# The first w_in part is converted between chunk 0's and chunk 1's steps, and the planner judges orders by five cases and another clock

## The chip, the core and the metric

The kernel runs on one core of one Trainium2 chip. The time is the device time of one execution in microseconds (us); the time of a version is the median of three executions. One further execution was recorded by the hardware profiler, and all views below come from it.

## What is computed

An attention block with a state per head (RWKV-7) feeds a two-layer network:

```python
# batch 4, heads 8, 768 tokens, head size 40; all float32
for t in range(S):
    y[:, :, t] = einsum('bhd,bhde->bhe', r_t, state)
    Sa = einsum('bhde,bhe->bhd', state, a_t)
    state = state * w_t[..., None, :] - outer(Sa, b_t) + outer(v_t, k_t)
x = y laid out as 3072 tokens x 320
h = x @ w_in                 # 320 x 2048, float64
out = (h * sigmoid(h)) @ w_out   # 2048 x 320, float64
```

The two weight matrices arrive as 64-bit floats, so the kernel has to turn them into float32 itself, out of their 32-bit halves.

## The kernel before

**Chunks.** The 768 tokens are cut into 12 chunks of 64. For each chunk `prepare` forms the decays by two scans on VectorE (L627, L645) and scales k, b and a by them (L654, L664); TensorE (PE) then makes two triangular products per head (L682) and turns the keys (L769). A triangular matrix has to be inverted per chunk. For chunks 0 to 2 `special` does that: the product goes to DRAM (`ms`) and back (`xs`), VectorE inverts 16 x 16 blocks with pairs of a multiply (L795) and a reduction (L796), the result goes through DRAM again (`zs`, L881) into the tile `mi` (L887, eight transfers), and PE finishes with L926, L913 and six groups of L958, each of which waits for a VectorE addition (L973). Later chunks are inverted in pairs by `inverse` and `merge` (L1039, L1068). `chain` solves for the chunk's updates (L1135, L1166), carries the state to the next chunk (L1223, L1239, L1111, L1121, L1196), `read` forms the chunk's output (L1269, L1281, L1308, L1323, L1334), and `moe` does the network for its 256 tokens: L1405 and L1418 against w_in, a SiLU on ScalarE (L1428), L1445 against w_out.

**Weights.** `weights(n)` converts one part of a weight matrix; parts 0 to 3 and the side tile `wi3` are w_in, the other five w_out. A part is fetched by GpSimd's queue (L479) into a borrowed buffer (`gts`, `wo`, `raw`, `XI`). VectorE and ScalarE then take the words apart: L484 (VectorE), L485 (ScalarE), L486 and L487 (VectorE), L488 (ScalarE). For the first three parts ScalarE also scales the low words (L502), PE adds the halves by four matmuls against the identity (L508), two trace matmuls for each, and VectorE multiplies the sum in (L520). The rest do the sum on VectorE (L493, L500). GpSimd's fetches are held back by small copies (L853) that wait for a given tile, so that loads come in a chosen order.

**Order.** Every step is added to a `Plan` with an engine, a cost, the tiles that it reads and writes, and a priority `pri` (lower is earlier). `Plan.order` lists the steps: at each point it takes the step that can start first, with `pri` weighed in. `Plan.best` draws ten settings and then tries 400 random shifts of priorities; each listing is judged by `Plan.through`, which walks it once per case of `CASES` and returns the end, and the listing with the smallest sum of ends is issued. Engines execute in that order, with semaphores between them; a step that waits holds everything behind it on its own engine. `through` also holds a model of how PE's instructions are fetched in blocks of 256 and of PE's clock by windows of 3.41 us. So a change to the cases or to one priority can shift any step of the whole program.

The priorities that matter here: chunk 0's inverse has -13 and its chain -12, chunk 1's `prepare` -8, its inverse -7, and weights have 1 and more.

Of the kernel before, what the change touches and what calls it, by code (L numbers as in the profile page):

```python
# [33 lines left out]
class Plan:  # L34
# [32 lines left out]
    RATE, LAND = 300.0, 2.0  # L67
    COLD = 42.0
    URGE = {"SP": 0.0, "ACT": 0.03, "PE": 0.05, "DVE": 0.1, "POOL": 0.02}
    LEAVE = {"F": 0.09, "R": 0.2, "T": 0.13, "Q": 0.13, "H": 0.12, "S": 0.11}  # L70
    ENTER = {"F": 0.08, "R": 0.1, "T": 0.03, "Q": 0.03, "H": 0.03, "S": 0.03}

    def turn(self, op):

        a, b = self.shape, op["shape"]
        if a == b or {a, b} == {"R", "T"}:
            return 0.03 if a != "F" else 0.0
        return self.LEAVE[a] + self.ENTER[b]

# [90 lines left out]
            out.append(op)  # L170
        return out

    SLOW = 2.8, 1.7
    CASES = (1.0, 300.0, 0.15, 1.0), (1.5, 240.0, 0.15, 1.0), (1.5, 240.0, 0.25, 1.04)
    WINDOW, FEW = 3.41, 0.42

    def through(self, out, crowd, rate, hop, slower):

        at = dict.fromkeys(self.HOP, 0.0)
        queue = dict.fromkeys(("SP", "ACT", "POOL"), 0.0)
        end, free = [0.0] * len(out), {}
        fetched, count, shape, work = [0.0, 0.0], 0, "Q", {}
        before, after = self.SLOW
        width, few = self.WINDOW, self.FEW
        for op in out:
            e = op["engine"]
            s = at[e]
            for b in op["before"]:  # L190
                s = max(s, end[b] + (hop if self.ops[b]["engine"] != e else 0.0))
            for place in op["takes"]:
                s = max(s, free.get(place, 0.0))
            if e == "PE":
                self.shape = shape
                t, shape = s + self.turn(op), op["shape"]
                to_ = count + op["k"]
                step = op["cost"] / op["k"]
                while count < to_:
                    block = count // 256  # L200
                    gate = 256 * block + 194
                    if len(fetched) == block + 1:
                        full = crowd if max(queue.values()) > t + 1 else 0.0
                        fetched.append(max(t + 0.4, fetched[-1] + before) + after + full)
                    if count >= gate:
                        t = max(t, fetched[-1] + 0.1)
                    to = min(to_, gate if count < gate else 256 * block + 256)
                    left, count = (to - count) * step, to
                    while left > 1e-9:
                        w = int(t / width)  # L210
                        pace = 0.5 if t > 30 and work.get(w - 1, 0.0) < few * width else 1.0
                        d = min((w + 1) * width - t + 1e-9, left / pace)
                        work[w] = work.get(w, 0.0) + d
                        t += d
                        left -= d * pace
            else:
                t = s + op["cost"] * (slower if e == "DVE" else 1.0)
            at[e] = t
            if op["size"]:
                begin, work_ = max(queue[e], t), op["size"] / rate  # L220
                both = max(0.0, max(queue[o] for o in queue if o != e) - begin)
                queue[e] = begin + (2 * work_ if work_ < both / 2 else work_ + both / 2)
                for o in queue:
                    if o != e and queue[o] > begin:
                        queue[o] += min(work_, both / 2)
                t = queue[e] + self.LAND
            end[op["n"]] = t
            for place in op["gives"]:
                free[place] = max(free.get(place, 0.0), t + 0.1)
        return max(end)  # L230

    def best(self, draws, steps):
# [10 lines left out]
        def value(urge, cold, moved):  # L243
# [12 lines left out]
            for op in out:  # L256
                for room in op["rooms"]:
# [4 lines left out]
                    op["gives"].append(place)  # L262
            spans = [self.through(out, *case) for case in self.CASES]
            return sum(spans), out, {i: room.slot for i, room in rooms.items()}
# [24 lines left out]
def kernel(  # L289
# [17 lines left out]
    B, S = v.shape[0], v.shape[1]  # L307
    D, H, P, Q = 40, 8, 4, 16
    DM, DF = w_in.shape[0], w_in.shape[1] // 2
    NF = DF // 128  # L310
    T = B * C
# [53 lines left out]
    few = ZQ.rearrange("p q t -> p (q t)")  # L365
# [8 lines left out]
    def vec(n):  # L374
        return 0.15 + n * 0.00104

    def act(n):
        return 0.19 + n * 0.00082
# [20 lines left out]
    def dma(do, size, r=(), w=(), pri=0, engine="SP", rooms=()):  # L399
        add(engine, 0.45, do, r, w, pri, rooms, size=size)  # L400
# [60 lines left out]
    def weights(n):  # L461
        dst, srcs, key = units[n]
        room = raw[places[n]].bitcast(I32)
        keys = held[places[n]]
        words = room.rearrange("p (c two) -> p c two", two=2)
        lo, hi = words[:, :, 0], words[:, :, 1]
        if len(dst.shape) == 3:
            lo, hi = (x.rearrange("p (k c) -> p k c", k=2) for x in (lo, hi))
        e = dst.bitcast(I32)
        shr, band, bor = ALU.logical_shift_right, ALU.bitwise_and, ALU.bitwise_or  # L470
        pri = (1 if n < 5 else 3) + 0.2 * n
        gate = gates[max(k for k in gates if k <= n)]
        by_pe = n < NP

        def fetch(rows_, src):
            to = room[rows_]
            if len(src.shape) == 3:
                to = to.rearrange("p (g c) -> p g c", g=src.shape[1])
            nc.gpsimd.dma_start(to, src)  # L479

        for n_, (rows_, src) in enumerate(srcs):
            dma(partial(fetch, rows_, src), 1024 / len(srcs), [("@", gate)], [*keys, ("raw", n, n_)], pri, "POOL")
        me = keys
        add("DVE", vec(512), lambda: nc.vector.tensor_scalar(out=e, in0=hi, scalar1=20, scalar2=0x7FF, op0=shr, op1=band), me, key, pri)  # L484
        add("ACT", act(WS), lambda: nc.scalar.activation(out=e, in_=e, func=AF.Relu, scale=2.0**23, bias=low), [], key, pri)  # L485
        add("DVE", vec(WS), lambda: nc.vector.scalar_tensor_tensor(out=e, in0=hi, scalar=-(1 << 31), in1=e, op0=band, op1=bor), me, key, pri)  # L486
        add("DVE", vec(512), lambda: nc.vector.tensor_scalar(out=hi, in0=hi, scalar1=0xFFFFF, scalar2=None, op0=band), [], me, pri)  # L487
        add("ACT", act(WS), lambda: nc.scalar.activation(out=hi.bitcast(F32), in_=hi, func=AF.Copy, scale=2.0**-20, bias=1.0), [], me, pri)  # L488
        if not by_pe:
            add(  # L490
                "DVE",
                vec(WS),
                lambda: nc.vector.scalar_tensor_tensor(  # L493
                    out=hi.bitcast(F32), in0=lo.bitcast(U32), scalar=2.0**-52, in1=hi.bitcast(F32), op0=ALU.mult, op1=ALU.add
                ),
                [],
                me,
                pri,
            )
            add("DVE", vec(WS), lambda: nc.vector.tensor_tensor(out=dst, in0=dst, in1=hi.bitcast(F32), op=ALU.mult), me, key, pri)  # L500
            return
        add("ACT", act(WS), lambda: nc.scalar.activation(out=lo.bitcast(F32), in_=lo.bitcast(U32), func=AF.Copy, scale=2.0**-52), [], me, pri)  # L502
        pf = Room("pair", 5, 1)
        for h in range(2):
            for i in (1, 0):

                def sum_(h=h, i=i):
                    nc.tensor.matmul(  # L508
                        pf.tile[:, h],
                        lhsT=ident,  # L510
                        rhs=words[:, 512 * h : 512 * h + 512, i].bitcast(F32),
                        start=i == 1,
                        stop=i == 0,
                    )

                add("PE", 0.86, sum_, me, [(pf, h)], pri, [pf], 2, shape="F")

        def product():
            f = pf.tile if len(dst.shape) == 3 else pf.tile.rearrange("p a b -> p (a b)")
            nc.vector.tensor_tensor(out=dst, in0=dst, in1=f, op=ALU.mult)  # L520

        add("DVE", vec(WS), product, [(pf, 0), (pf, 1)], key, pri, [pf])
# [955 lines left out]
    for n in range(5):  # L1478
        weights(n)
# [24 lines left out]
    with tc.manual_schedule():  # L1504
# [5 lines left out]
    count = sb.tile([128, 1], F32, name="count")  # L1510
# [7 lines left out]
        out=bad, in0=pb[0:1, 0:1], scalar1=128.0 * 2 * NN - 0.5, scalar2=None, op0=ALU.is_lt  # L1518
# [9 lines left out]
    with tc.If(flag > 0):  # L1528
# [24 lines left out]
        T = 16  # L1553
        with tc.For_i(0, S, T) as t0:
# [3 lines left out]
            for dg in range(4):  # L1558
                for b in range(B):
                    L = slice(32 * dg + H * b, 32 * dg + H * b + H)  # L1560
# [26 lines left out]
        with tc.For_i(0, B * S, 128) as t0:  # L1587
# [12 lines left out]
            for f in range(NF):  # L1600
                ph = gps.tile([128, 512], F32, name="gph", bufs=2)
                F = slice(f * 128, f * 128 + 128)
# [57 lines left out]
```

## Time and profile before

| | |
|---|---|
| median of 3 executions | 743.88 us (742.13 to 744.6) |
| the profiled execution's own time | 742.53 us |
| its span in the profile | 740.8 us |
| mean granted TensorE clock | 0.976 |
| busy: PE, VectorE (DVE), ScalarE (ACT), GpSimd (POOL) | 674.7, 419.5, 194.6, 14.3 us |
| chain that ended last, share of PE | 80% |

PE is busy for 91% of the span. Its rows are listed as time, duration, line, tile and count; an `issue` behind "idle before" is a wait for nothing that the profile shows. A row of PE's shows two matmuls for one matmul of the program, and one for a transpose (L769, L926, L1196), and as many weight loads (PEld). The row `PEclk` is the clock that was granted, as a share of full speed.

### The profile page before, as it was taken

To read this page: it belongs to the slowest core of one execution; us is meant where nothing else is said; L and a number is where in the kernel's file an instruction comes from. 1 tells how busy PE (TensorE), PEld (TensorE's weight loads), DVE (VectorE), ACT (ScalarE), POOL (GpSimd) and SP (SyncE) were. 2 spreads that over 40 slices of the span, in tenths; PEclk is the share of its full clock that TensorE was granted. 3 is DMA by queue.
4 is the path that set the end of the run, shared out by engine and by line. 5 is a ranking of instruction groups with operands and counts; after the bars stand their busy time and mean duration, and the time that the engine had idled before them with its cause. 6 is when DMAs were issued, how large, how long until landed. Compare 5 with 4: busy or idle time off the path is not lost.

```text
span 740.8 us, 27279 instructions
## 1 busy us (share of the span) xinstructions
PE 674.7 (91%) x12666; PEld 540.5 (73%) x12666; DVE 419.5 (57%) x614; ACT 194.6 (26%) x241; POOL 14.3 (2%) x31
## 2 busy tenths in 40 slices
PE   2179799898899999999999999899999999999995
PEld 2176577678678677878778878778777778788773
DVE  6845799976479256299273397362686449321000
ACT  3251635523212411404304205124114211202020
POOL 2300000000000000000000000000000000000000
PEclk9996999999999999999999999999998999999998
DMA  7770654742632453525353506333233321401000
GB/s 248 160 227 11 195 210 126 222 116 47 161 107 58 96 135 98 139 61 125 112 133 106 161 19 144 95 99 92 73 93 81 97 60 32 126 21 41 18 1 22
DMA packets 117979, 77.15 MB, mean 104 GB/s; under 512 B 65506, under 2 KB 114338, under 8 KB 117218
## 3 DMA queue, kind: packets, MB, share of 16 engines
q1 hardware_dynamic: 113352, 64.54, 32.9%
q0 software_dynamic: 2096, 10.49, 4.3%
q8 instruction: 101, 1.65, 0.9%
q10 hardware_dynamic: 2410, 0.30, 0.3%
q14 instruction: 20, 0.16, 0.1%
HBM read 60.29 MB, written 14.61 MB: 101 GB/s over the span
## 4 chain that ended last, share of the span: by engine, by line
PE 80%; DVE 8%; DMA 3%; ACT 3%; issue 3%; SPq 1%; ACTq 1%; DVEq 0%
PE pair L1445 27%; PE pair L1405 21%; PE pair L1418 5%; PE pair L1269 4%; PE pair L682 3%; PE pair L1323 3%; PE pair L958 2%; PE pair L1135 2%; PE pair L1223 2%; PE pair L1068 1%; PE pair L1166 1%; PE pair L508 1%; PE pair L744 1%; PE pair L1308 1%; PE pair L1111 1%
## 5 line engine op out<-in xcount | busy, mean ns | idle before, releaser
L1445 PE MATMUL pair<-wo,gts 128*128 128x320 f32 x768 | 219.8, 442 | 1.1 <-issue 1.1
L1445 PEld LDWEIGHTS pair<-wo,gts 128*128 128x128 f32 x768 | 144.7, 192 | 60.4 <-issue 4.3
L1405 PE MATMUL pair<-xt,wi 128*128 128x256 f32 x768 | 175.5, 386 | 1.6 <-ACT R L756 1.3
L1405 PEld LDWEIGHTS pair<-xt,wi 128*128 128x128 f32 x768 | 145.7, 192 | 24.5 <-ACT R L756 1.4
L1428 ACT ACTIVATE gts<-pair 128x1024 f32<-128x1024 f32 x48 | 46.5, 1020 | 134.5 <-PE pair L1418 108.3
L682 PE MATMUL pair<-a,kb 40*64 40x64 f32 x1536 | 32.2, 236 | 35.8 <-DVE a L654 28.7
L1457 DVE COPY ot<-pair 128x320 f32<-128x320 f32 x24 | 11.8, 490 | 92.4 <-PE pair L1445 88.9
L796 DVE TENSOR_REDUCE XI<-XI 128x64 f32<-128x512 f32 (+9 forms) x85 | 58.6, 690 | 2.9
L682 PEld LDWEIGHTS pair<-a,kb 40*64 40x64 f32 x1536 | 28.6, 149 | 38.5 <-issue 20.5
L1418 PE MATMUL pair<-xt,wi 64*128 64x256 f32 x384 | 47.9, 389 | 0.0
L1281 DVE TENSOR_TENSOR lam<-pair,ml 128x1024 f32<-128x1024 f32 x22 | 26.4, 1220 | 32.9 <-PE pair L1269 30.4
L1418 PEld LDWEIGHTS pair<-xt,wi 64*128 64x128 f32 x384 | 35.1, 187 | 6.7 <-issue 2.6
L795 DVE TENSOR_TENSOR XI<-XI,mi 128x1024 f32<-128x1024 f32 (+8 forms) x60 | 33.6, 559 | 9.6 <-DMA mi<-md 8.3
L1334 DVE TENSOR_TENSOR lam<-pair,wz 128x1024 f32<-128x1024 f32 x11 | 13.5, 1223 | 38.8 <-PE pair L1323 38.8
L1269 PEld LDWEIGHTS pair<-r,vut 40*64 40x64 f32 x1536 | 25.9, 142 | 6.8 <-issue 5.9
L664 DVE TENSOR_TENSOR kb<-kbv 128x512 f32<-128x512 f32 (+1 forms) x36 | 29.7, 861 | 0.3
L1269 PE MATMUL pair<-r,vut 40*64 40x64 f32 x1536 | 28.5, 228 | 1.2 <-issue 1.2
L627 DVE TENSOR_TENSOR_SCAN kbv<-wz,zt 128x1024 f32<-128x1024 f32 x12 | 27.5, 2291 | 0.5
L645 DVE TENSOR_TENSOR_SCAN wz<-wz,zt 128x1024 f32<-128x1024 f32 x12 | 27.5, 2289 | 0.3
L756 ACT COPY R<-pair 128x640 f32<-128x640 f32 x12 | 8.3, 693 | 67.1 <-PE pair L744 61.5
L795 DVE TENSOR_TENSOR XI<-XI,xs 128x1024 f32<-128x1024 f32 (+1 forms) x25 | 25.3, 1010 | 0.8
L407 ACT ACTIVATE vu<-pair 64x640 f32<-64x640 f32 x13 | 9.1, 698 | 60.3 <-PE pair L1135 59.4
(151 smaller groups left out, 687.7 us busy)
## 6 DMA issues: line engine op xcount, KB each, us to landing
wz<-in_wT SPq DMA_DIRECT2D x12, 512.0 KB
kbv<-in_bT SPq DMA_DIRECT2D x12, 512.0 KB
a<-in_aT SPq DMA_DIRECT2D x12, 512.0 KB
kbv<-in_kT SPq DMA_DIRECT2D x12, 512.0 KB
r<-in_rT SPq DMA_DIRECT2D x48, 96.0 KB
vut<-in_vT SPq DMA_DIRECT2D x48, 96.0 KB
vu<-in_v SPq DMA_DIRECT2D x24, 160.0 KB
out<-ot SPq DMA_DIRECT2D x48, 80.0 KB
```

The costliest lines, as they stand in the source:

```text
L627: nc.vector.tensor_tensor_scan(back(V), back(W[:, 2 : 2 + Q * C]), zt, 1.0, ALU.mult, ALU.add)
L645: nc.vector.tensor_tensor_scan(Z, Z, zt, 0.0, ALU.mult, ALU.add)
L664: TTn[engine].tensor_tensor(out=at_(kb, place(is_b, first), (576 * step, 4 // step), (128, 4), (1, C)), in0=blocks((kf, bf)[is_b]), in1=bl ...
L682: nc.tensor.matmul(room.tile[half(b), j, g * C : g * C + C], lhsT=kb[rows(j), place(is_b, q) : place(is_b, q) + C], rhs=A[rows(j), q * C : ...
L795: nc.vector.tensor_tensor(out=at_(tmp, 0, *dims), in0=x, in1=y, op=ALU.mult)
L796: nc.vector.tensor_reduce(out=out_, in_=at_(tmp, 0, *dims), axis=AX.X, op=ALU.add)
L1269: nc.tensor.matmul(pl.tile[half(1 - b if role else b), b, c * C : c * C + C], lhsT=vut[rows(b), role, hu, :], rhs=rs[rows(b), hh, :], star ...
L1281: lambda pl=pl, la=la: nc.vector.tensor_tensor(out=la.tile.rearrange("p (q t) -> p q t", q=Q), in0=pl.tile.rearrange("p a b -> p (a b)").r ...
L1405: nc.tensor.matmul(rooms[g].tile[:, f // 2, (f % 2) * T : (f % 2) * T + T], lhsT=wi[:, k, (4 * g + f) * 128 : (4 * g + f) * 128 + 128], rh ...
L1418: nc.tensor.matmul(rooms[g].tile[:, h, (f % 2) * T : (f % 2) * T + T], lhsT=wi3[half(h), g * 256 + (f % 2) * 128 : g * 256 + (f % 2) * 128 ...
L1428: nc.scalar.activation(out=gts[:, 4 * g * T : 4 * g * T + 4 * T], in_=rooms[g].tile.rearrange("p a b -> p (a b)"), func=AF.Silu)
L1445: nc.tensor.matmul(po[b].tile[:, 0, 0:DM], lhsT=g4[:, f, 128 * b : 128 * b + 128], rhs=wo[:, f, :], start=f == 0, stop=f == NF - 1,)
```

## The change

`weights(0)` gets the priority -8.5 in place of 1: behind chunk 0's steps (-13 to -12) and ahead of chunk 1's `prepare` (-8). The planner's cases go from three to five; each now carries its own two times for fetching PE's instructions, the crowding, the transfer rate, the hop between engines and VectorE's factor. The clock in `through` changes: it now starts at half speed, a window counts at half for work done at half speed, and the share of a window that must be worked is 0.48 to be raised and 0.38 to be kept up, where it was 0.42 of the window before, whatever the clock. Two shapes get a cost for a change of shape that no step here uses.

The kernel does the same operations on the same data; only the order of the engines' instructions differs, over the whole program. On PE one of the four additions of w_in's first part (L508) now stands ahead of chunk 0's L926; three stand behind the chain's L1166 and L1269. The four of the second part stand together behind L1223.

```diff
-    LEAVE = {"F": 0.09, "R": 0.2, "T": 0.13, "Q": 0.13, "H": 0.12, "S": 0.11}
-    ENTER = {"F": 0.08, "R": 0.1, "T": 0.03, "Q": 0.03, "H": 0.03, "S": 0.03}
+    LEAVE = {"F": 0.09, "R": 0.2, "T": 0.13, "Q": 0.13, "H": 0.12, "S": 0.11, "L": 0.13}
+    ENTER = {"F": 0.08, "R": 0.1, "T": 0.03, "Q": 0.03, "H": 0.03, "S": 0.03, "L": 0.03}
...
-    SLOW = 2.8, 1.7
-    CASES = (1.0, 300.0, 0.15, 1.0), (1.5, 240.0, 0.15, 1.0), (1.5, 240.0, 0.25, 1.04)
-    WINDOW, FEW = 3.41, 0.42
-
-    def through(self, out, crowd, rate, hop, slower):
+    CASES = (
+        (2.8, 1.3, 1.0, 300.0, 0.15, 1.0),
+        (2.8, 1.3, 1.0, 300.0, 0.25, 1.0),
+        (2.0, 1.9, 1.0, 240.0, 0.25, 1.0),
+        (2.0, 1.9, 2.0, 240.0, 0.15, 1.0),
+        (1.4, 1.3, 3.0, 300.0, 0.35, 1.05),
+    )
+    WINDOW, FEW = 3.41, (0.38, 0.48)
+
+    def through(self, out, before, after, crowd, rate, hop, slower):
...
-        fetched, count, shape, work = [0.0, 0.0], 0, "Q", {}
-        before, after = self.SLOW
+        fetched, count, shape = [0.0, 0.0], 0, "Q"
+        window, work, pace = -1, 0.0, 0.5
...
-                        pace = 0.5 if t > 30 and work.get(w - 1, 0.0) < few * width else 1.0
+                        if w > window:
+                            known = w == window + 1 and work >= few[pace < 1.0] * width
+                            window, work, pace = w, 0.0, 1.0 if known else 0.5
                         d = min((w + 1) * width - t + 1e-9, left / pace)
-                        work[w] = work.get(w, 0.0) + d
+                        work += d * pace
...
-        pri = (1 if n < 5 else 3) + 0.2 * n
+        pri = -8.5 if n == 0 else (1 if n < 5 else 3) + 0.2 * n
```

The instructions' order on each engine follows from the two programs as they are built; the prediction speaks of these orders. PE, in the first 80 us of before (counts of the program's matmuls): L682 x32 x2, L769 x16 x2, L744 x32, **L682 x32**, L926, L913, **L769 x16**, L958 x16 six times, L1166 x16, L682 x32, L1166 x16, **L769 x16**, L508, L1269 x32 x2, L508 x2, L1323, L1135, L508, L744, L1223, L1196, L1111, L1405 x8. PE after: L682 x32 x2, L769 x16 x2, L744 x32, **L508**, L926, L913, L958 x16 six times, L1166 x16, L682 x32, **L508**, L1166 x16, L1269, L508 x2, L1269, L1135, **L769 x16 x2**, L1323, L1223, **L508 x4**, L682 x32, L1111, L1196, L744, L1405 x8. (Lines are those of the kernel before.)

On VectorE, w_in part 0's L486 and L487 come right behind the last L796 of chunk 0's inverse and ahead of chunk 1's L633 to L664. On ScalarE, L488 comes ahead of the four transfers L887 that ScalarE issues, and L502 right behind them. VectorE's L795 and L796 of chunk 1's inverse, begun before the chain's products in the kernel before, all come behind L1239. On SP's queue, the transfer `zs` (L881) of chunk 1 comes behind eight loads of r and vut and one of a, where it stood behind four loads of r and vut.

## The prediction

> **What bounds the kernel now.** I read the page first: the slices of PE and of its clock.
>
> ```profile
> PE   2179799898899999999999999899999999999995
> PEclk9996999999999999999999999999998999999998
> ```
>
> A slice is 18.5 us. PE is nearly idle in the first two and full from the fifth on, so the end is set by PE's work plus what PE loses, and most of the loss lies ahead of 90 us. The order listings show the same matmuls in both programs; a gain can only be less idle time or less time at half clock. Next the timeline of PE, from where the long idle time ends:
>
> ```profile
> 36.15 1.99 PE L682 MATMUL pair<-a,kb 40*64 40x64 f32 x64 [14.93 <-DVE a L654]
> 38.06 1.12 PE L926 MATMUL pair<-ident,mi 64*128 64x64 f32 x16
> ...
> 46.48 3.31 PE L958 MATMUL pair<-XI 64*64 64x64 f32 x102 [0.99 <-issue]
> 49.65 0.64 PE L1166 MATMUL pair<-X,R 64*40 64x64 f32 x26
> 53.04 0.26 PE L1166 MATMUL pair<-X,R 64*40 64x64 f32 x3 [2.76 <-issue]
> ...
> 56.88 2.07 PE L508 MATMUL pair<-gts,ident 128*128 128x512 f32 x2
> ...
> 74.24 0.60 PE L1196 MATMUL pair<-ident,G 40*104 40x40 f32 x16 [0.92 <-DVE G L1239]
> 77.24 5.33 PE L1405 MATMUL pair<-xt,wi 128*128 128x256 f32 x16 [1.32 <-ACT R L756]
> ```
>
> Two stops have nothing behind them that the profile shows ("issue"). Ahead of the first PE has run 474 matmuls, ahead of the second 602: 128 apart, 256 instructions with the weight loads. So I read them as the fetch of PE's program in blocks of 256. The windows, with the granted clock in the third number from the end, show what the second stop does:
>
> ```profile
> 50.00:53.00 3.00, 0.28 (x18) 0.13 (x6) 0.52 (x1) 0.00 (x0) 0.00 (x0) 1.00 0.36 48
> 53.00:57.00 4.00, 3.96 (x119) 3.72 (x119) 2.99 (x6) 1.20 (x3) 0.00 (x0) 0.53 0.15 37
> 57.00:62.00 5.00, 5.00 (x118) 3.50 (x122) 1.41 (x4) 0.69 (x1) 0.00 (x0) 0.50 0.01 3
> 62.00:67.00 5.00, 5.00 (x46) 2.33 (x40) 3.35 (x11) 0.00 (x0) 0.00 (x0) 0.51 0.01 3
> 77.00:81.00 4.00, 3.76 (x10) 3.05 (x11) 3.75 (x5) 1.85 (x3) 0.00 (x0) 0.57 0.74 210
> ```
>
> PE is full from 54 to 67 us, but at half clock: 13.7 us (53.2 to 66.9), and 3.4 us more after the waits at 74 and 76 us. The four matmuls L508 at 62.50 (two adds) stand right ahead of the return. Last the timelines of VectorE and ScalarE for the steps that the change moves:
>
> ```profile
> 29.83 0.69 DVE L796 TENSOR_REDUCE ZQ<-XI 128x64 f32<-128x512 f32 x1
> 37.75 1.22 DVE L486 SCALAR_TENSOR_TENSOR wi<-gts,wi 128x1024 int32<-128x1024 int32 x1
> 39.00 0.70 DVE L487 TENSOR_SCALAR gts<-gts 128x1024 int32<-128x1024 int32 x1
> ```
>
> ```profile
> 32.36 1.85 ACTq L887 DMA_DIRECT2D mi<-zs  x4
> 43.27 1.15 ACT L488 ACTIVATE gts<-gts 128x1024 f32<-128x1024 int32 x1
> 44.32 1.14 ACT L502 ACTIVATE gts<-gts 128x1024 f32<-128x1024 uint32 x1
> ```
>
> **Step 1, the head of chunk 0's inverse: +0.3 us.** Out of PE's way go L682 (1.99) and a later L769 (1.08), in comes one L508 (2.07 at this clock). But ScalarE now has L488 ahead of the `mi` transfers. L796 ends at 30.5; L486 and L487 follow (1.22 + 0.70), to 32.4; L488 ends at 33.6 in place of an issue at 32.36. The four issues last 1.85, to 35.5, L502 1.14, to 36.6; L508 waits for it and ends at 38.7. Behind L508 are queued L926 and the whole inverse. `mi` itself lands 1.9 after its last issue (as `ms` did: 18.38 to 20.26), at 37, and is not what ends last. L926 starts at 38.7, not 38.06. The gap that L769 filled shrinks, though ScalarE's L675 (1.06 + 0.18) now stands between the copies of X and XI; L958 starts near 42.3, not 42.03. Bounds: -1 if that L508 runs at full clock, +2 if a transfer is late. VectorE's chunk 1 work moves 1.9 later, into its idle 4.0 us ahead of L973; without that cover it would cost the 1.9.
>
> **Step 2, the stops for instructions: -1.1.** The blocks' borders fall elsewhere: what was matmul 474, a third into the L958s, is now matmul 168 of their 192; 602 is in the second L1166. Before, from the end of one block's use (matmul 346, near 40.4) to the release at 46.48 it took 6.1, and from there to 53.04 6.6, while transfers kept the 16 DMA engines full. Now matmul 346 is the 40th of L958, at 43.7; release 49.8. PE is there near 48.2 (168 matmuls in 5.9, by the old pace without its stop): a stop of 1.6. The next point comes after 0.8 + 0.6 + 1.1 + 1.0 + 0.1 of work, at 53.4; the transfers are done by then (0.44 busy at 50 to 52), so I take 54.4: a stop of 1.0, with 0 and 3.0 (the old 6.6) as bounds. Sum 2.6 against 0.99 + 2.76.
>
> [...]
>
> **Step 3, the half clock behind them: -1.7.** A stop of 1.6 in work of small matmuls will, I think, still bring the clock down. Before, the clock came back when two adds (four L508 matmuls) filled most of 3.4 us. Now a single add and then a pair stand earlier, ahead of the second L1269, and should bring it back one such stretch earlier: half of 3.4. Bounds: -6.8 if it is never lost (half of 13.7), +3.1 if it only comes back with the four adds behind L1223 near 73 us (half of 6.1).
>
> [...]
>
> **Step 4, 72 to 82 us: -3.8.** Behind L1223 PE waits 0.92 for G and 1.32 for R, and the following L1405 runs at half clock for 3.4 us (5.33 for 16, against 3.72 at 102.06): 0.92 + 1.32 + 1.6. Four adds (4.1) now stand there, with L682, L1111, L1196 and L744 behind: 4.1 + 1.14 + 1.14 + 0.6 + 1.14 = 8.1 of work against the 6.5 that xt needs (L1334's end at 70.76 to 77.24). So the cover is there, and with it no low window. L744 needs VectorE's L729, behind L1239 and the small inverse steps: 0.8 + 3.2 + 0.2 + 1.4 + 1.2 = 6.8, within the 7.0 ahead of it. Bounds -3.9 and -1.0 (L744 late by 1.2 and a dip of the clock).
>
> **Step 5, chunk 1's inverse: +1.5.** Its small steps now start behind L1239, and on SP `zs` is queued behind nine loads. SP needs 4.9 for xt and 9 x 0.49 for the loads: `zs` goes out near 79.8 against 77.84, and `mi` lands 9.8 later (as 77.84 to 87.6), at 89.6. Behind it waits L913 and the chain of chunk 1. PE has four adds more done by then (4.1), which are its cover to near 88; 1.6 to 2.5 of waiting against the 0.97 of before (0.54 + 0.43 ahead of L913). Bounds 0 and +3.
>
> **The rest: 0, within 3 either way.** Behind 120 us the waits of PE listed in the timeline sum to 17 us, most of them "issue". Between L1135 and L1223 only 1.1 us of filler stands in four of eleven chunks before and in five now (a wait of 0.77 each, by the row at 183.27), and between L1039 and L1068 mostly 2 us or more in both. VectorE, nearly full from 100 to 140 us, has about 5 us of weight work done earlier, which helps if anything.
>
> Sum: 0.3 - 1.1 - 1.7 - 3.8 + 1.5 = -4.8 on the profiled execution's 742.53, so 737.7. That execution is 1.35 below the median; on 743.88 it gives 739.1.
>
> **The rivals.**
> *The clock stays up.* The stops become short and spread, no window is light, and step 3 is -6.8 in place of -1.7: -9.9, 734.0. For it: the longest stop halves by step 2. Against it: at 73 to 77 us two waits of about 1 us were enough to lose the clock.
> *Slower: the clock comes late.* In the trace the L958s speed up from 43 us (64 in 2.49, then 102 in 3.31): the clock was first granted there, behind L926, L913 and L769 without a gap. If the new wait ahead of L926 leaves that stretch too light, the L958s and what follows run at half clock until the four adds: +5.1 for 43 to 53.2, +3.1 as in step 3, the stops hide in it (-2.6 in place of -1.1), step 4 shrinks to -2.4, steps 1 and 5 stay: +5.0, 748.9. It decides if L958 still takes 39 ns each in its second half.
> *No gain.* The early gain is there, but PE is only a few us ahead when chunk 1's inverse ends (step 5 at +3), and the later order loses 2 to 3 us in stops: about 743.
>
> **Chances.** Forecast 0.40, clock up 0.14, no gain 0.20, clock late (or a worse later order) 0.26. A change within 0.3% (2.2 us) can't be told from none; so faster 0.54, same 0.20, slower 0.26. The range reaches to the two clock rivals, with their ends cut a little: 731.5 to 748.5.
>
> **What would show it.** Right: L508 as two matmuls ahead of L926, L926 between 38 and 39.5; stops ahead of the last L958 and not in the first L1166; full clock again before 64 us; no wait ahead of L1196 and L1405; `zs` of chunk 1 near 80 us and a wait ahead of L913. Wrong: L1405 of chunk 0 starting after 80 us, or PE behind by 120 us, or a change that only grows behind 200 us.

## The result, and the profile after

The changed kernel takes 747.92 us (740.62 to 753.46, 22 runs), the kernel before, run beside it, 740.59 us (736.53 to 749.28, 22 runs). The ratio is 1.009, with a 95% interval of 1.0065 to 1.0114: slower, where faster was forecast. In a second set of runs it was 746.17 us against 742.45 us, 1.0036 (1.0 to 1.0073). So the change costs some 4 to 7 us.

The ratios here leave out runs of a kernel that lie over 1.5% above its fastest, and since each of these kernels spreads by 2%, a ratio can stand below that of the medians; both are given.

The page's PE rows, as shown for before:

```profile
span 746.0 us, 27285 instructions
PE   2389798998899989999999999999999999999995
PEclk9999999899999999998999999999999899999998
```

The second and third slices are fuller than before (3 and 8, where they had 1 and 7). Behind them PE's rows hardly differ, but the clock's row, which before dipped in the fourth slice and the thirty-first, now dips in the eighth, the nineteenth and the thirty-second. The timeline of PE up to 92 us:

```profile
33.59 2.07 PE L516 MATMUL pair<-gts,ident 128*128 128x512 f32 x2 [12.38 <-ACT gts L496]
35.93 1.31 PE L934 MATMUL pair<-ident,mi 64*128 64x64 f32 x16 [0.26 <-DMA mi<-zs]
...
40.87 3.68 PE L966 MATMUL pair<-X,XI 64*64 64x64 f32 x64 [1.72 <-ACT XI L413]
...
52.46 0.58 PE L1174 MATMUL pair<-X,R 64*40 64x64 f32 x25 [0.37 <-issue]
...
71.55 3.72 PE L1413 MATMUL pair<-xt,wi 128*128 128x256 f32 x16
...
81.04 0.30 PE L921 MATMUL pair<-mi,sb 64*64 64x64 f32 x2 [1.26 <-DMA mi<-zs]
83.16 1.94 PE L921 MATMUL pair<-mi,sb 64*64 64x64 f32 x62 [1.83 <-DMA mi<-zs]
```

(Lines of the changed kernel are 8 above those of before: L516 is the addition L508, L921 is L913, L966 is L958, L1413 is L1405, L690 is L682.) The stop of 2.76 us is 0.37, and L1413 starts at 71.55 in place of 77.24 and needs 3.72 in place of 5.33. Then come two waits for `mi` of chunk 1. The windows over the stretch that had been at half clock:

```profile
50.00:57.00 7.00, 6.63 (x225) 4.22 (x217) 3.76 (x5) 5.16 (x6) 0.00 (x0) 1.00 0.18 27
57.00:64.00 7.00, 5.66 (x230) 5.40 (x221) 5.56 (x6) 2.56 (x4) 0.00 (x0) 1.00 0.11 26
```

Before, these two windows were:

```profile
50.00:57.00 7.00, 4.24 (x137) 3.85 (x125) 3.52 (x7) 1.20 (x3) 0.00 (x0) 0.73 0.24 42
57.00:64.00 7.00, 7.00 (x132) 4.71 (x133) 2.96 (x6) 0.69 (x1) 0.00 (x0) 0.50 0.02 5
```

PE now runs 455 matmuls in them where it ran 269. The clock was granted later (at 45.7 us by the trace's clock record; 43.0 before) but then held until 83.25. By these two profiles, the change does more up to here than was forecast.

But much of that is not the change's doing. Four profiles have the old order up to this point: before, and the experiments e4, e6 and e12 that are told below. The long half clock of before (13.65 us from 53.22) is in e4 too (13.65 us from 51.96). In e6 there are 3.4 us of it, from 47.97, and in e12 none between 42 and 72.8 us, although PE stopped for 1.55 and 2.21 us at the same matmuls as before. e12:

```profile
46.91 3.31 PE L1047 MATMUL pair<-XI 64*64 64x64 f32 x102 [1.55 <-issue]
...
52.94 0.26 PE L1255 MATMUL pair<-X,R 64*40 64x64 f32 x3 [2.21 <-issue]
...
72.57 5.38 PE L1494 MATMUL pair<-xt,wi 128*128 128x256 f32 x16 [0.68 <-DVE wi L609]
```

```profile
57.00:64.00 7.00, 6.92 (x244) 5.38 (x244) 5.20 (x18) 0.00 (x0) 0.00 (x0) 1.00 0.02 5
```

(L1047 is L958 of before, L1255 is L1166, L1494 is L1405.) Chunk 0's first L1405 starts at 77.24 and 76.95 us in before and e4, at 72.23 and 72.57 in e6 and e12, and at 71.55 to 72.74 in three profiles of the changed kernel. So most of the 5.7 us by which the changed kernel's profile is ahead here is also what one execution of the kernel before has on another. The waits ahead of L1405 and the half clock over it, which the change removes, are in all four.

Further on in the changed kernel:

```profile
122.16 0.73 PE L690 MATMUL pair<-a,kb 40*64 40x64 f32 x33
126.34 0.69 PE L690 MATMUL pair<-a,kb 40*64 40x64 f32 x31 [3.44 <-issue]
...
138.07 0.88 PE L1316 MATMUL pair<-r,GT 40*40 40x64 f32 x24 [1.33 <-issue]
```

```profile
120.00:126.00 6.00, 2.90 (x120) 2.61 (x110) 5.67 (x7) 4.26 (x6) 0.00 (x0) 1.00 0.84 182
126.00:134.00 8.00, 7.66 (x95) 5.33 (x95) 5.15 (x6) 4.16 (x5) 0.00 (x0) 0.60 0.54 149
```

PE is idle for half of the first of these windows and at a clock of 0.60 in the second; before, these two windows had 5.74 and 7.43 us of PE at a clock of 1.00. And behind 190 us PE stops for 0.9 us or more six times (8.8 us), where it did three times before (5.0 us). Two of the six:

```profile
197.11 0.68 PE L690 MATMUL pair<-a,kb 40*64 40x64 f32 x29 [1.95 <-issue]
...
516.53 0.73 PE L1316 MATMUL pair<-r,GT 40*40 40x64 f32 x24 [1.49 <-issue]
```

The longest of before's three stands near the first of these, the second is new:

```profile
198.79 0.69 PE L682 MATMUL pair<-a,kb 40*64 40x64 f32 x31 [2.77 <-issue]
```

**The lead.** To place the loss I added up, for each profile, the work that PE has done by a time: each group of matmuls counts with its duration at full clock, however long it took. The table is the lead over the profile of before, in us. The last six rows belong to experiments told below.

| profile | 80 us | 90 | 120 | 140 | 190 | 725 |
|---|---|---|---|---|---|---|
| after | +9.6 | +5.2 | +6.3 | +0.4 | +0.2 | -7.1 |
| after, second profile (e9) | +9.3 | +4.9 | +4.7 | -0.5 | -2.3 | -6.4 |
| after, third profile (e17) | +9.2 | +4.7 | +5.5 | +0.5 | -2.6 | -5.1 |
| e3, old order behind chunk 0 | +8.6 | +4.1 | +2.4 | -2.5 | -4.0 | -3.2 |
| e7, `zs` earlier | +7.5 | +5.8 | +5.9 | +0.5 | -1.4 | -2.6 |
| e8, loads later | +9.7 | +4.9 | +5.6 | +2.9 | +2.3 | +3.4 |
| e10, both | +6.8 | +5.3 | +6.3 | +3.3 | +2.6 | -3.5 |
| e11, both, old late order | +8.1 | +6.5 | +6.8 | +6.1 | +6.6 | +8.0 |
| e18, as e11 | +8.2 | +6.2 | +6.9 | +7.8 | +5.8 | +5.6 |

So a lead of 9 us is there at 80 us, some 4.4 of it go within ten us, 5 more between 120 and 140, and the rest, and more, behind 190. The lead counts from one execution of the kernel before: reckoned in the same way, e6 and e12, with the old order, are themselves some 4 us ahead at 80 us. So how a row changes says more than how high it stands. From 190 to 725 us the six rows with the changed late order (after, e9, e17, e7, e8, e10) change by -7.3 to +1.1, on average by -3.4, and the three with the old late order (e3, e11, e18) by -0.2 to +1.4, on average by +0.7.

### The profile page after: what moved, and what is told of

Same layout as the page of the kernel before. It is cut to its first block, busy times and chain, and to the rows that moved or that the text cites. A ratio compares the mean times of both kernels' runs of the same rounds, so it can differ in the third digit from the quotient of the medians.

```text
span 746.0 us, 27285 instructions
## 1 busy us (share of the span) xinstructions
PE 679.1 (91%) x12666; PEld 543.1 (73%) x12666; DVE 419.2 (56%) x614; ACT 194.7 (26%) x241; POOL 14.8 (2%) x31
## 4 chain that ended last, share of the span: by engine, by line
PE 75%; DVE 11%; DMA 5%; issue 4%; SPq 2%; ACT 2%; ACTq 0%; DVEq 0%
PE pair L1453 26%; PE pair L1413 19%; PE pair L1426 5%; PE pair L1277 3%; PE pair L690 3%; PE pair L1331 3%; PE pair L1231 2%; DVE XI L803 2%; PE pair L966 2%; PE pair L1143 1%; PE pair L1174 1%; PE pair L1076 1%; DVE kbv L635 1%; PE pair L1316 1%; DVE XI L804 1%
## 5 line engine op out<-in xcount | busy, mean ns | idle before, releaser
L1453 PE MATMUL pair<-wo,gts 128*128 128x320 f32 x768 | 222.4, 446 | 1.4 <-issue 1.4
L1453 PEld LDWEIGHTS pair<-wo,gts 128*128 128x128 f32 x768 | 146.2, 194 | 61.9 <-issue 6.3
L1413 PE MATMUL pair<-xt,wi 128*128 128x256 f32 x768 | 176.9, 387 | 1.0 <-DVE R L1129 0.5
L1413 PEld LDWEIGHTS pair<-xt,wi 128*128 128x128 f32 x768 | 145.8, 193 | 23.7 <-DVE R L1129 0.9
L690 PE MATMUL pair<-a,kb 40*64 40x64 f32 x1536 | 30.5, 232 | 22.2 <-DVE a L662 13.8
L1289 DVE TENSOR_TENSOR lam<-pair,ml 128x1024 f32<-128x1024 f32 x22 | 26.4, 1220 | 36.6 <-PE pair L1277 23.8
L690 PEld LDWEIGHTS pair<-a,kb 40*64 40x64 f32 x1536 | 27.4, 145 | 25.7 <-issue 23.6
L1277 PEld LDWEIGHTS pair<-r,vut 40*64 40x64 f32 x1536 | 24.3, 135 | 5.7 <-issue 4.0
L1277 PE MATMUL pair<-r,vut 40*64 40x64 f32 x1536 | 27.0, 220 | 0.0
L1231 PE MATMUL pair<-vu,kt 128*40 128x40 f32 x704 | 17.7, 213 | 6.1 <-DVE vu L419 3.0
```

The costliest lines, as they stand in the source:

```text
L690: nc.tensor.matmul(room.tile[half(b), j, g * C : g * C + C], lhsT=kb[rows(j), place(is_b, q) : place(is_b, q) + C], rhs=A[rows(j), q * C : ...
L1231: nc.tensor.matmul(pg.tile[rows(j), b, c * D : c * D + D], lhsT=K[:, 8 * b + c, j], rhs=vu[:, b, h], start=True, stop=True,)
L1277: nc.tensor.matmul(pl.tile[half(1 - b if role else b), b, c * C : c * C + C], lhsT=vut[rows(b), role, hu, :], rhs=rs[rows(b), hh, :], star ...
L1413: nc.tensor.matmul(rooms[g].tile[:, f // 2, (f % 2) * T : (f % 2) * T + T], lhsT=wi[:, k, (4 * g + f) * 128 : (4 * g + f) * 128 + 128], rh ...
L1453: nc.tensor.matmul(po[b].tile[:, 0, 0:DM], lhsT=g4[:, f, 128 * b : 128 * b + 128], rhs=wo[:, f, :], start=f == 0, stop=f == NF - 1,)
```

## The experiments

All eighteen stand in one table; times are medians, each beside runs of the kernel before on the same chip.

| run | us (range, runs) | before | ratio (95%) |
|---|---|---|---|
| e1 priority only | 750.06 (745.78 to 752.03, 7) | 742.91 | 1.0108 (1.0068 to 1.0148) |
| e2 cases and clock only | 742.2 (735.03 to 748.23, 12) | 742.91 | 0.9985 (0.9944 to 1.0025) |
| e3 changed head, old order behind | 745.77 (739.92 to 752.37, 12) | 742.91 | 1.003 (0.9995 to 1.0065) |
| e4 old head, changed order behind | 749.71 (738.12 to 758.25, 12) | 742.91 | 1.0059 (1.0011 to 1.0108) |
| e5 changed order to 190 us | 744.49 (741.64 to 749.56, 12) | 742.44 | 1.0037 (1.0002 to 1.0072) |
| e6 changed order from 190 us | 747.2 (740.71 to 753.41, 12) | 742.44 | 1.0024 (0.9981 to 1.0068) |
| e7 `zs` earlier | 744.76 (737.78 to 748.09, 12) | 742.44 | 1.0042 (1.0006 to 1.0078) |
| e8 loads later | 743.78 (738.48 to 751.21, 12) | 742.44 | 1.003 (0.9995 to 1.0066) |
| e9 the changed kernel | 746.17 (739.35 to 753.04, 12) | 742.45 | 1.0036 (1.0 to 1.0073) |
| e10 e7 and e8 | 739.96 (734.96 to 745.72, 12) | 742.45 | 0.9982 (0.9945 to 1.0018) |
| e11 e10, old order from 190 us | 737.09 (731.72 to 742.59, 12) | 742.45 | 0.9945 (0.9907 to 0.9984) |
| e12 before, loads bunched | 745.1 (733.93 to 751.02, 12) | 742.45 | 0.9977 (0.9926 to 1.0029) |
| e13 to e16 dummies, 36 blocks (e14: 72) | 1034.63 to 1354.19 (6 each) | 742.31 | see below |
| e17 after, one block of dummies | 746.41 (740.55 to 748.32, 6) | 738.03 | 1.0107 (1.0061 to 1.0153) |
| e18 e11, one block of dummies | 734.01 (727.76 to 738.49, 12) | 738.03 | 0.9939 (0.9899 to 0.9979) |

In e3 and later runs the order of steps is written out as a list in the kernel, which moves its lines by 81 against the changed kernel (L1002 is L921, L771 is L690, L1397 is L1316, L597 is L516); e9, e13, e14 and e17 keep the planner. In the first four expectations theory A says that the early gain is there and the order behind it, drawn anew, loses more; B that the moved part itself costs; C that the new cases choose worse orders; D that the lead is only borrowed work.

**e1 and e2: which part of the edit.**

```diff
# e1: the kernel before with
+        pri = -8.5 if n == 0 else (1 if n < 5 else 3) + 0.2 * n
# e2: the changed kernel with
+        pri = (1 if n < 5 else 3) + 0.2 * n
```

> Only the priority of the first w_in part is changed; the planner keeps its three cases and its old clock. Theory A (the early part of the new order gains about 6 us, and the order behind 120 us, which the planner draws anew, loses more than that): the early gain is there if one addition of w_in's first part again stands ahead of chunk 0's L926 and the clock is up at 57 us, and the end is another draw of the later order: 735 to 748, not told by A more closely. Theory B (the moved part itself costs the time, through something it holds up all the way): 746 to 749, like the changed kernel, against about 740.6 before.

> Only the planner's cases and its clock are changed; the first w_in part keeps its old priority. Theory A: the later order is again a draw, 738 to 750, and the half-clock time behind 120 us in the profile (13.6 us before, 34.1 us changed) tells which. Theory B (the moved part costs the time): as before, 740 to 742. Theory C (the new cases choose worse orders): 746 to 750.

The priority alone gives the whole loss; the cases and the clock alone give nothing that can be told from the kernel before. C falls. A and B are not told apart by this, since the planner draws the whole order anew for the priority alone too. The profile of e1 has the same two places as the changed kernel: waits of 1.75 and 1.78 us for `mi` at 84 and 86 us, and a stop of 2.93 us that ends at 131.02.

**e3 and e4: head and tail.** In e3 the steps go in the changed order up to chunk 0's first L1445, some 300 of 1449, and then in the old order; e4 is the reverse.

> The issue order is written out: the changed kernel's order up to chunk 0's first L1445 (near 116 us), then the order of the kernel before for all that is left (the two heads differ by three steps). Theory A: the lead of some 6 to 7 us at that point is kept, 733 to 736 against 740.6 before. Rival D (the lead is only work drawn ahead, and is given back whatever follows): 740 to 742. Theory B: 746 to 749.

> The reverse: the order of the kernel before up to chunk 0's first L1445, then the changed kernel's order. Theory A: no early gain and all the later losses, 12 us or so: 750 to 754. Rival D: 746 to 748, like the changed kernel. Theory B: about 741.

e3 misses A's time, and e4 is slower, though less than A has it: by the medians there is loss on both sides of the cut, though e3's interval includes no change. The lead of e3 goes from 8.6 to 4.1 between 80 and 90 us, as after's does, and from 2.4 to -2.5 by 140; from there it changes by 1.5 us at most. Its stop near 128 us has another cause than after's. VectorE and ScalarE hold each other up there, as I read it because the old order puts weight steps ahead of the chain's:

```profile
126.82 1.22 DVE L575 SCALAR_TENSOR_TENSOR wo<-wo 128x1024 int32<-128x1024 int32 x1 [3.12 <-ACT wo L574]
128.08 0.69 DVE L576 TENSOR_SCALAR wo<-wo 128x1024 int32<-128x1024 int32 x1
128.69 1.22 DVE L753 TENSOR_TENSOR kb<-kbv 128x1024 f32<-128x1024 f32 x1
```

PE's L771 needs `kb` of that L753 and starts at 130.05, after 3.47 us. By this reading an order that suits PE at one pace does not suit it some us earlier; no run tests it alone.

**e5 and e6: a cut at 190 us.** At step 455 (about 190 us) both orders have issued the same set of steps, so the cut leaves each side as it was. From here on theory A is that the loss lies ahead of 190 us, T that it lies behind.

> The changed kernel's order for its first 455 steps (up to about 190 us, where both orders have issued the same set of steps), the old order behind that. Theory A (the early gain is given back at the waits near 82 and 126 us and the half clock behind them, all ahead of 190 us): still slow, 745 to 748 us. Theory T (the order behind 190 us is what costs): the early part is neutral, 740 to 743 us.

> The old order for the first 455 steps, the changed kernel's order behind that. Theory A: as the kernel before, 741 to 744 us. Theory T: 746 to 750 us. The sum of the differences of this run and the one before it should give the changed kernel's +5 to +7 us.

Neither holds alone: 2.1 us by the medians ahead of the cut, 4.8 behind it, 6.9 together, against 7.3 and 3.7 for the changed kernel in its two sets of runs. The ratios add less (1.0037 and 1.0024), and that of e6 does not exclude no change; that the order behind 190 us costs rests on the medians and on the lead's change there.

**e7: the first place, `mi` of chunk 1.** SyncE's queue in the changed kernel:

```profile
72.25 0.43 SPq L609 DMA_DIRECT2D vut<-in_vT  x1
72.78 0.40 SPq L573 DMA_DIRECT2D a<-in_aT  x1
73.30 0.42 SPq L889 DMA_DIRECT2D zs<-ZQ  x1
77.48 4.12 SPq L895 DMA_DIRECT2D mi<-zs  x8
```

`zs` goes out right behind eight loads and 512 KB of `a`, and the first `mi`, which waits for it to land, 4.2 us later; before, four of the loads and `a` came behind `zs`, and `mi` followed 2.9 us after it (77.84 to 80.75). VectorE had the sum for `zs` ready at 71.72. The edit to the order, three moves:

```diff
-SP: r vut r vut r vut r vut a(512 KB) zs mi x8
+SP: r r r r zs mi x8 vut vut vut vut a(512 KB)
-PE: L516 x6, L921 x64, L516 x2
+PE: L516 x8, L921 x64
```

> The changed kernel, with three moves near 72 us only: zs of chunk 1 goes out on SyncE as soon as its sum is there, ahead of the four vut loads and the 512 KB load of a, which now stand behind the mi transfers; and the add of two L516 matmuls that stood behind the waiting L921 stands ahead of it. Theory A: the waits of 1.26 and 1.83 us ahead of L921 shrink to 1 us or less in sum and the half clock behind 83 us goes: 3 to 5 us less, 743 to 745 us. Theory T: the time saved there is lost behind, no change, 747 to 749 us.

```profile
79.55 3.96 PE L597 MATMUL pair<-wo,ident 128*128 128x512 f32 x8 [0.45 <-ACT wo L577]
83.44 1.31 PE L1002 MATMUL pair<-mi,sb 64*64 64x64 f32 x64
```

The waits are gone. The time, 2.3 us above before by the medians, where the changed kernel is 7.3 and 3.7 us above, says little, since the intervals overlap. By the lead 1.7 us are lost between 80 and 90 us in place of 4.4 to 4.5, and 1.5 to 2.0 in e10, e11 and e18, which have the same moves. But these four are 1.0 to 2.8 us less far ahead at 80 us; at 90 us they stand at 5.3 to 6.5 against 4.7 to 5.2, so the moves are worth about 1 us. `zs` itself left no earlier than in the changed kernel (74.56 against 73.30). The first `mi` followed it after 2.1 us in place of 4.2, and PE came later to the place, at 83.44 in place of 79.77, two moved L516 included. The half clock did not go: it comes at 87.6 in place of 83.25, for the same 3.4 us, beside waits of 1.17 and 1.23 us for ScalarE's copies.

**e8: the second place, the stop at 122.9 us.** In the changed kernel SyncE sends all eight r and vut loads of chunk 2 from 116.16 to 120.00, then the eight `ms` from 121.42 on. The transfer that fetches PE's next block (16 KB, on queue q8, of kind `instruction`) starts at 123.41 and takes 1.54 us (0.97 for the one before it, at 113.44); PE goes on at 126.34.

```diff
-SP: r vut r vut r vut r vut, ms x8, xh xh
+SP: r, ms x8, vut r vut r vut, xh xh, r vut
```

> The changed kernel, with seven of chunk 2's r and vut loads moved on SyncE from ahead of the eight ms transfers near 116 us to behind them, as in the old order; nothing else differs. Theory A: the transfers of PE's program no longer fall in full DMA engines, the stop of 3.44 us at 122.9 us goes and with it the half clock at 127.6 us: 4 to 6 us less, 742 to 744 us. If the stop is there whatever the loads do (the block's border alone): 747 to 749 us.

```profile
122.82 0.73 PE L771 MATMUL pair<-a,kb 40*64 40x64 f32 x33
123.96 0.69 PE L771 MATMUL pair<-a,kb 40*64 40x64 f32 x31 [0.40 <-issue]
...
134.26 1.70 PE L1397 MATMUL pair<-r,GT 40*40 40x64 f32 x58 [2.96 <-DMA r<-in_rT]
```

```profile
120.00:126.00 6.00, 5.37 (x224) 4.89 (x219) 5.70 (x6) 4.93 (x8) 0.00 (x0) 1.00 0.43 133
```

The fetch starts at 121.57 and takes 0.90, with the DMA engines 0.43 busy in this window where they were 0.84; the stop at the same matmul, the 34th of that L771, is 0.40 in place of 3.44, and the half clock at 127.6 is gone. A new wait of 2.96 for `r`, whose load is now late, takes part of it back: the lead falls by 2.7 between 120 and 140, in place of 5.9, 5.2 and 5.0 in the three profiles of the changed kernel. By the medians e8 is 1.3 us above before.

**e9 to e12: together.** A says that the two costs add, L that the lead can't be kept. e11 takes the old order behind step 455 and sends the three late `r` ahead of the `vut`; e12 gives the kernel before the changed kernel's bunch of loads.

> The changed kernel itself, so that the next three stand against it on the same chip. Both theories: 746 to 749 us, 0.9% above the kernel before.

> The changed kernel with both sets of moves, those of the run that sent zs earlier and those of the run that put chunk 2's loads behind the ms transfers; all else in the changed kernel's order. Theory A, the two costs add (each took off 3 to 4 us alone): 739 to 741 us, some 2 us below the kernel before. Theory L (the early lead cannot be kept, one wait replaces another): 743 to 745 us, no better than either set alone.

> As the run before it, but with the old order behind the first 455 steps (some 190 us), and with chunk 2's three r loads ahead of the four vut loads behind the ms transfers, because in the trace of the single set PE waited 2.96 us for r at 134 us. Theory A: 737 to 740 us, the lowest of all. Theory L: 742 to 744 us.

> The kernel before, with one thing taken over from the changed kernel: chunk 2's seven r and vut loads stand on SyncE ahead of the eight ms transfers. Theory A: a stop for instructions of 2 to 3.5 us and half clock appear near 130 us, 3 to 5 us more than before, 745 to 747 us. If the loads only hurt where PE's block border happens to fall beside them: as before, 741 to 743 us.

e10 and e11 came as A has them: 6.2 us and 9.1 us below the changed kernel on the same chip. e11 is faster than both kernels, 0.9945 (0.9907 to 0.9984). Its PE in the first place and the second, where the wait for `r` is gone and a stop of 1.27 for `issue` stands at the same matmuls:

```profile
79.36 3.96 PE L597 MATMUL pair<-wo,ident 128*128 128x512 f32 x8 [0.45 <-ACT wo L577]
...
123.91 0.69 PE L771 MATMUL pair<-a,kb 40*64 40x64 f32 x32 [0.38 <-issue]
...
134.34 0.55 PE L1397 MATMUL pair<-r,GT 40*40 40x64 f32 x24 [1.27 <-issue]
```

e12 is a miss for A and not conclusive: the median is 2.7 us above before, the ratio 0.9977 (0.9926 to 1.0029), and its profile has no stop of 2 us near 130. The border between the two blocks of PE's program falls beside the loads there too, at the same instruction as in the changed kernel (4288, counted as below), and the fetch for it started late: 3.3 us behind the border before it, against 3.8 in the changed kernel and 1.3 in e8. But by the old order PE needs 5.9 us for that block, with an L1445 in it, where the changed order has 3.3 us of work. As I read it, the loads cost much only where the block is also short.

e11 differs from e10 in two things, the late order and the place of the three `r`: the lead at 140 us is 6.1 against 3.3, so not all of the 2.9 us between them is the late order's.

**e13 to e18: the borders of the blocks.** Every wait of PE over 0.9 us with `issue` behind it, 130 in the twenty profiles of this case, ends at instruction 193 or 194 of a block of 256 (counted over PE's matmuls, weight loads and semaphore instructions), and 0.96 to 1.62 us behind the landing of a fetch. In sixteen of the profiles I took the 1394 borders behind 90 us: where PE had used the block in under 2.6 us, a wait of over 0.3 stood at 90 of 135; between 2.6 and 4.4 us, at 62 of 401; above, at 11 of 858. Theory F says that the borders' places make the late stops, O that the late order does. Dummy matmuls at the start were to move the borders by half a block:

```diff
+for _ in range(64):   # and 128 in e14
+    nc.tensor.matmul(pairs[0][0:40, 0, 0:40], lhsT=zt[0:64, 1:41], rhs=zt[0:64, 1:41], start=True, stop=True)
```

> The changed kernel with 64 dummy matmuls (128 PE instructions with their weight loads) near 4 us, where PE is idle; their output is zero and used nowhere. Theory F (a stop stands at each block border, instruction 193 of 256, behind which PE used the block in less than about 3 us): with the borders half a block further on, the sum over the borders behind 90 us of what each block falls short of 3.1 us goes from 10.6 to 3.9 us, the stops at 197, 470, 516 and 577 us go, and the kernel takes 738 to 743 us. Theory O (the late order itself makes them): stops stay with the same matmuls, 746 to 748 us.

> The same with 128 dummy matmuls, 256 instructions: all borders fall on the same matmuls as in the changed kernel. Both theories: 746 to 748 us, the stops where they were (it costs nothing else, since the dummies end ahead of PE's first work at 13.8 us).

> The kernel before with the 64 dummy matmuls. Theory F: the sum goes from 14.3 to 6.8 us, stops at 198, 272 and 465 us go, others of up to 1 us may come; 735 to 739 us. Theory O: 741 to 743 us.

> The kernel with both sets of moves and the old late order (737 us) with the 64 dummy matmuls. Theory F: the sum goes from 11.7 to 5.1 us; 730 to 734 us. Theory O: 736 to 738 us. In either case the lowest of all, if the gains add.

> The changed kernel with 64 dummy matmuls once, 128 PE instructions near 4 us; output zero and used nowhere. Theory F: the stops at order positions 4290, 7105, 14530, 17089, 19138 and 20929 go; stops stand at positions 65 of 256 instead, and the blocks' shortfall behind 90 us is 3.9 us in place of 10.6; 738 to 743 us. Theory O: the stops stay with the same matmuls; 746 to 748 us.

> The kernel with both sets of moves and the old late order (737 us) with the 64 dummy matmuls once. Theory F: shortfall 5.1 us in place of 11.7; 730 to 734 us, the lowest of all. Theory O: 736 to 738 us.

No border moved in any of the six, and that was my error twice. In e13 to e16 the loop stood in a function that is called 36 times, not once, and I had forgotten that one matmul of the program is two in the trace, with two weight loads: 64 of them are 256 instructions, one whole block, in e17 and e18, and 36 blocks in e13. So the six are controls. The first real matmul moves from 13.79 to 310.64 us in e13; without these 296.9 us its 1045.14 is 748.3, and e14 (604.1 us later) 750.1: the changed kernel's time. e16 is 737.8, e11's time; e15 is 745.6, 3.3 us above the kernel before, for which I have no cause. Likewise the stops stay at the same instructions, 9216 (36 blocks) or 256 further on. Two of them in e13, the same matmuls as at 126.34 and 197.11 in the changed kernel, though the loads of the program's start had landed 300 us before; chunk 2's eight loads stand ahead of the first of the two here too (413.67 to 417.62 us):

```profile
423.32 0.69 PE L690 MATMUL pair<-a,kb 40*64 40x64 f32 x31 [2.89 <-issue]
...
495.77 0.69 PE L690 MATMUL pair<-a,kb 40*64 40x64 f32 x29 [3.08 <-issue]
```

What the controls say is that the stops belong to the order and are not chance in their places; their lengths vary (1.84 us in e14 where e13 has 2.89). F against O stays open; an order with its borders moved was not run. What the profiles do show is the size: behind 190 us the eight profiles with the changed late order (after, e4, e6 to e10, e17) have PE waits of 0.9 us or more that sum to 8.1 us on average, the six with the old one (before, e3, e5, e11, e12, e18) 4.0 us; half clock between 190 and 700 us lasts 17.5 against 12.0 us, which costs half of its length (in before two L508 matmuls took 2.07 us at a clock of 0.50, from 56.88; in the changed kernel two L516 of the same shape took 1.06 at full clock, from 78.72). That is 4.1 and 2.8 us more, enough to cover the 4.8 by e6's median and e10's 2.9 above e11; it is an account of where the time goes, not a test of why. e18 shows the gain of e11 a second time, on another chip: 0.9939 (0.9899 to 0.9979).

## Why the prediction was wrong

The step that failed is "The rest: 0". Over the profile that it was worked out from, the changed kernel leads by 4.7 to 5.2 us at 90 us, which is the forecast's 4.8. That the sum fits is in part luck: more was gained by steps 2 and 3 than forecast, and more lost by step 5. What was put at 0 behind 90 us then took back all of it and more; at 725 us the lead is -5.1 to -7.1.

**Step 1 (+0.3):** near. L516 did not wait for L510 (L502), only for L496, and started at 33.59, not 36.6; L934 ran at 35.93, not 38.7. Most of that went into the 1.72 us that L966 waited for ScalarE's copy of XI, and half clock to 45.7: by 50 us the lead was -0.2.

**Step 2 (-1.1):** right in the places of the two stops, which came out smaller. The second and third profiles have the first stop, 1.41 at 49.92 and 1.62 at 50.03, against 1.6 at 49.8 by the prediction, and not the second; the first profile has only the second, 0.37 at 52.46, against 1.0. At 60 and 65 us two further stops of 0.28 to 0.99 stand, which the prediction doesn't have.

**Step 3 (-1.7):** the rival "the clock stays up" was right here. The clock held from about 46 us to 83 in all three profiles, in two of them across a stop of 1.4 to 1.6 us. But both the step and the rival set out from 13.7 us of half clock, and that is in only two of the four profiles with the old order; so not all of it was there to be gained, and some 4 us of the lead of 9 come from the choice of that one profile.

**Step 4 (-3.8):** right, L1413 with no wait ahead and at full clock. The waits and the half clock that it priced are in all four profiles with the old order. The first four steps summed to -6.3; the lead at 80 us is 9.2 to 9.6 over the profile of before, and some 5 over e6 and e12.

**Step 5 (+1.5):** mis-sized, in PE's cover and not in the transfers. `zs` left at 73.30, not 79.8, because PE and the `xt` transfers were earlier, and from there to the end of the last wait for `mi`, at 83.16, it took 9.86, where 9.8 was forecast. But PE was earlier still: forecast to have work to near 88, it had none from 79.77. In place of 1.6 to 2.5 less the old 0.97 it waited 3.09, a half clock of 3.4 us (1.7) followed, and the lead fell by 4.4.

**The rest (0, within 3):** this step failed. Its reasons were averages over chunks (waits of 0.77, filler of 1.1 us), and the loss is at single places: 5 to 6 us between 120 and 140, of which e8, e10 and e11 give back 2.0 to 5.2 by SyncE's order alone, and some 4 behind 190, by the lead's change and e6's median. Why the order behind 190 us costs stays open beyond its stops and half clock. The trace of before has 20.0 us of PE waits behind 120 us, 10.3 of them `issue`, not 17 that are mostly so. PE's stops at block borders were read rightly for the first 90 us and then not carried through the other 1150 steps, although their positions (193 of 256) could be counted from the listing.

Of the rivals, "slower" ended on the right side by the wrong mechanism: the clock came 2.7 us later in the first profile, not 10, and 3.5 us earlier in the second. Its half sentence "or a worse later order" was what happened. "No gain" named the two places but gave them 2 to 3 us.

The blocks that step 2 reads off two stops can be counted in the trace of before as well: queue q8, of kind `instruction`, has 101 transfers of 16 KB, for PE's 25332 matmuls and weight loads and 107 semaphore instructions, 252 for each. A wait of over 0.3 us stood at 163 of the 1394 borders: 1231 had none, and the stop at 126.34 us in the changed kernel was 3.44. Step 3 has the clock come back when two adds filled most of 3.4 us. Many dips last just 3.4 us (three of the five ahead of 735 us in before, the others 6.83 and 13.65), but the second profile of the changed kernel has such a stretch that is full and is followed by another at half clock:

```profile
131.70:135.10 3.40, 3.40 (x36) 2.65 (x35) 0.25 (x1) 3.06 (x5) 0.00 (x0) 0.50 0.83 232
135.10:138.50 3.40, 3.40 (x30) 1.95 (x32) 3.24 (x4) 1.10 (x2) 0.00 (x0) 0.50 0.42 131
```

So what brings the clock back was not shown. The windows of 3.41 us and the shares 0.42, 0.38 and 0.48 in `through` are constants of the planner; the traces have dips of that length, and none of them shows the shares.

## What to carry to other kernels

Here a lead on the bottleneck engine was worth only what the queues behind it could feed (9.6 us at 80 us, 5.2 at 90, with 3.09 us of waits for `mi` between): after each gain, look up what the engine waits for next, and in which order that queue (here SyncE's) sends it. When a planner is free to draw the whole order again, price the new order to its end, block borders included, or keep the old one behind the place that changed; here the change with two reordered groups of loads and the old order from 190 us on is 0.55% faster where the change alone is 0.4 to 0.9% slower. When a kernel's times spread by 2%, as here, price a change against several profiles of the kernel before: one had 13.7 us of half clock that another, with the same order, had not. And count the instructions that an experiment adds in the trace's units before running it.

## What the runs showed of the hardware

- PE's program came in blocks of 256 instructions (101 transfers of 16 KB in before, 252 of its instructions for each); all 130 `issue` waits over 0.9 us ended at place 193 or 194 of a block, nearly all 1.2 to 1.6 us behind the landing of a fetch of about 1 us (median 1.06). A block used in under 2.6 us ended in a wait of over 0.3 us at 90 of 135 borders, one used in more than 4.4 us at 11 of 858.
- With the DMA engines 0.84 busy, in the changed kernel, a fetch started later and took longer (123.41 us and 1.54) than with 0.43, in e8 (121.57 and 0.90). In e12, with 0.94, it also started late, 3.3 us behind the border before it, but took 0.93.
- The times of one kernel with one order spread by 2% (735.31 to 751.13 us for the kernel before, 34 runs). Its half clock differs from run to run: near 50 us it lasted 13.65, 13.65 and 3.4 us in three profiles with the old order and was not there in a fourth, which had stops of 1.55 and 2.21 us. Behind 128 us it lasted 6.8, 10.2 and 10.2 us in three profiles of the changed kernel.
